# The end of an attention-and-spectral kernel: the last four row blocks copied and stored by ScalarE alone

## The chip, the core and the metric

The kernel runs on one core of a Trainium2 chip. A core has five engines that run side by side: TensorE (PE, matrix products), VectorE (DVE), ScalarE (ACT), GpSimd (POOL) and SyncE (SP, which here only issues DMA transfers and waits). Each engine works through its own list of instructions in order, and semaphores hold an engine back until another engine or a transfer has finished. The metric is device time in microseconds (us) for one execution of the whole program; lower is better.

## What is computed

The output has 2048 rows of 896 columns. The left 448 columns are multi-query attention, the right 448 a filter in the frequency domain:

```python
# A: 16 heads of 28, one key head and one value head
q = (x @ wq) split into heads;  k = x @ wk;  v = x @ wv
p = softmax(q @ k.T * 28 ** -0.5)
a = concat_heads(p @ v) @ wo                       # 2048 x 448
# B: 2-D real FFT, product with a complex filter, inverse
b = irfft2(rfft2(x) * (w_r + 1j * w_i))            # 2048 x 448
return concatenate([a, b], axis=-1)
```

## The kernel before

Attention is taken in four chunks of 512 query rows (`NC = 4`, `CW = 512`), in each chunk in four groups of four heads (`NG = 4`), and for each group over 16 blocks of 128 keys. A long list of steps, `PLAN`, sets by hand how scores (L891), exponentials (L826, L902, L916) and products with the values (L837) follow each other, and which pieces of the spectral half lie between them. The order of the instructions on PE, DVE and ACT is the order of the program's text in this part; SP's transfers stand in the order in which their data are made.

An output projection follows each chunk: a chunk's 512 rows are four row blocks of 128, and a row block's 128 x 448 result is a sum of products over the four head groups in one PSUM bank. For accuracy each factor is kept as a high and a low part, so that a group costs three products: high x high, low x high, high x low. For the first three chunks this work is spread through `PLAN`. The last chunk (`c = 3`) has nothing behind it, and its projection is the end of the program:

- `flush(kept)` (L948) makes the last products with the values; DVE transposes the result (L841).
- A loop over the four row blocks (L950 to L956) divides by the softmax sums and makes the high and low parts of the last head group, on DVE.
- `partial(k)` (L935) issues row block k's nine products over the head groups 0 to 2 (L745), which need nothing of that loop. `final(k)` (L939) issues its three products over group 3 (L942 to L944) and then calls `wo_out`.
- The order is partial 0, partial 1, final 0, partial 2, final 1, partial 3, final 2, final 3 (L957 to L963).
- `wo_out` (L747) copies the result from PSUM to an SBUF tile and stores it. With `last` from 1 to 3 (row blocks 0 to 2 here) ACT copies all 448 columns (L753) and SP issues the store (L757). With `last` 4 (row block 3) the columns are cut in two halves of 224: ACT copies the first and issues its store itself, DVE copies the second (L755) and SP issues that store.
- The SBUF tile `yb` has the tag `p0` or `p1` by turns, with one buffer each. So the copy of row block 2 must wait until the store of row block 0 has landed, and the copy of row block 3 until that of row block 1 has.

Behind this stands a branch (L968, L969): each of the five engines loads one number (`bits`, a bound on the scores, long known by then) into a register, compares it, and jumps over a slower fallback, L970 to L1035, which these data don't need. Behind the jump each engine waits for its own last work, and SP for all transfers and all engines, before the program ends (these instructions carry L969 and L1153).

Of the kernel before, what the change touches and what calls it, by code (L numbers as in the profile page):

```python
# [14 lines left out]
AF = mybir.ActivationFunctionType  # L15
# [5 lines left out]
S, D, H = 2048, 448, 16  # L21
# [48 lines left out]
def kernel(ctx: ExitStack, tc: tile.TileContext, t: dict):  # L70
    nc = tc.nc
# [73 lines left out]
    def fft1_a_mm(q, p):  # L145
        f, cs1 = ff[q], fc["cs1"][:113]
        pa = pair_of(bank())
        for e in range(2):
            for k, (n, o0) in enumerate(((113, 0), (112, 113))):
                for h in range(2):  # L150
                    for r in range(2):
                        r0 = 64 * h + 32 * r
                        mm(pa[r0:r0 + 32, e, o0:o0 + n], f[:, 2 * r + k, 2 * p + e, h], cs1[:, 2 * r + k, :n],  # L153
                           start=True, stop=True)
        return pa

    def fft1_a_out(q, p, pa):
        a = at1[q, p] = fp.tile([128, 2, DF], F32, name="a", tag=("pwr", "pwi")[p])
        return nc.scalar.activation(a, pa, AF.Copy)

    def fft1_b(q):
        return fft1_out(q, fft1_mm(q))
# [92 lines left out]
    with tc.tile_pool(name="w1", bufs=1) as w1:  # L255
# [37 lines left out]
        with tc.tile_pool(name="x1", bufs=2) as x1:  # L293
# [63 lines left out]
            def evac(c, g, pq):  # L357
                cs = slice(c * CW, (c + 1) * CW)
                out = nc.scalar.activation(qraw[:, g, cs], pq, AF.Copy)
                nc.vector.tensor_reduce(qmx[:, g, c:c + 1], qraw[:, g, cs], axis=AX.X, op=ALU.max,  # L360
                                        apply_absolute_value=True)
                return out
# [55 lines left out]
            for c in range(1, NC):  # L418
                for g in range(NG):
# [3 lines left out]
                    last = evac(c, g, pq)  # L423
# [43 lines left out]
        for p in range(2):  # L467
            last = fft1_a_out(6, p, fft1_a_mm(6, p))
# [7 lines left out]
        last = fft1_b(5)  # L476
# [26 lines left out]
    d, f, a, b, e, c = free  # L503
# [6 lines left out]
    def take():  # L510
        ready, bank = free.pop(free.index(min(free, key=lambda x: x[0])))
        clock["pe"] = max(clock["pe"], ready + 100)
        return bank
# [32 lines left out]
    def at_once(work=640, engine="dve"):  # L546
        clock[engine] = max(clock[engine], clock["pe"] + 200) + work
# [191 lines left out]
    def wo_mm(p, c, k, gs):  # L739
        s = slice(k * 128, k * 128 + 128)  # L740
        for g in gs:
            for n, (x, w) in enumerate(((oh, woh[:, g]), (ol, wox[:, g - 1] if g else woh[:, 0]), (oh, wol[:, g]))):
                if n == 1 and g == 0 and c < NC - 1:
                    continue
                mm(p, x[c][:, g, s], w, start=(g == 0 and n == 0), stop=(g == NG - 1 and n == 2))  # L745

    def wo_out(p, c, k, last=0):  # L747
        y = pp.tile([128, D], F32, name="yb", tag=f"p{k % 2}") if last else ap.tile([128, D], F32, name="ya")
        r0 = c * CW + k * 128
        for e in ((0, 1) if last == 4 else (0,)):  # L750
            s = slice(e * D // 2, (e + 1) * D // 2) if last == 4 else slice(0, D)
            if last and not e:
                nc.scalar.activation(y[:, s], p[:, s], AF.Copy)  # L753
            else:
                nc.vector.tensor_copy(y[:, s], p[:, s])  # L755
                at_once()
            (nc.scalar if last == 4 and not e else nc.sync).dma_start(t["oa"][r0:r0 + 128, s], y[:, s])  # L757

    wps = {}

    def wo_unit(c, k, g):
        if g == 0:
            wps[c, k] = take()
        p = wps[c, k][:, :D]
        need(("o", c, g))
        for x in (g,) if g == 0 else (g, g + NG - 1):
            need(("wo", x))
        wo_mm(p, c, k, (g,))
        passed(600 if g else 400)
        if g == NG - 1:  # L770
            wo_out(p, c, k)
            give(wps.pop((c, k)))
# [95 lines left out]
    for tokens in PLAN:  # L868
# [10 lines left out]
        for k in tokens:  # L879
# [9 lines left out]
            c, g, kc = steps[i if kind == "-" else n - 1 - i]  # L889
# [21 lines left out]
        for i in reversed(range(stay)):  # L911
# [5 lines left out]
            else:  # L917
                for h in hs:
                    p = keep[i][h // 2][:, h % 2]
# [12 lines left out]
    c = NC - 1  # L932
    ws = []

    def partial(k):  # L935
        ws.append(take()[:, :D])
        wo_mm(ws[k], c, k, range(NG - 1))

    def final(k):  # L939
        p, s = ws[k], slice(128 * k, 128 * k + 128)  # L940
        h, l = oh[c][:, NG - 1, s], ol[c][:, NG - 1, s]
        mm(p, h, woh[:, NG - 1], start=False, stop=False)  # L942
        mm(p, l, wox[:, NG - 2], start=False, stop=False)
        mm(p, h, wol[:, NG - 1], start=False, stop=True)  # L944
        wo_out(p, c, k, k + 1)


    flush(kept)  # L948
# [1 line left out]
    for k in range(4):  # L950
        divide(c, NG - 1, k)
        s = slice(128 * k, 128 * k + 128)
# [3 lines left out]
        nc.vector.tensor_tensor(ol[c][:, NG - 1, s], on[:, s], h.bitcast(F32), op=ALU.subtract)  # L956
    for k in (0, 1):  # L957
        partial(k)
    for k in (2, 3):
        final(k - 2)  # L960
        partial(k)
    final(2)
    final(3)  # L963


# [3 lines left out]
    with tc.If(rv > int(np.float32(BOUND).view(np.int32))), tc.tile_pool(name="g1", bufs=1) as g1:  # L969
# [32 lines left out]
        oa = t["oa"].rearrange("(n p) d -> n p d", p=128)  # L1002
        with tc.For_i(0, NC, 1) as nq:
            y = g1.tile([128, 4, D], F32, name="y")
            nc.vector.memset(y, 0.0)
            with tc.For_i(0, NG, 1) as ng:
# [5 lines left out]
                for i in range(4):  # L1012
# [3 lines left out]
                    with tc.For_i(0, 16, 1) as nk:  # L1016
# [5 lines left out]
                        p = g1.tile([128, CW], F32, name="pe")  # L1022
# [134 lines left out]
```

## Time and profile before

| | |
|---|---|
| median of three runs | 641.0 us (640.72 to 641.24) |
| the profiled execution | 640.4 us |
| its span, from the first to the last instruction | 638.6 us |
| busy time PE / ACT / DVE / POOL | 630.2 / 547.4 / 416.9 / 79.8 us |
| granted TensorE clock over the span | 0.998 of full speed |
| DMA traffic | 66.76 MB, 105 GB/s on average |

The page gives the busy time of each engine, the span in 40 slices, the chain of work that ended last, and the costliest groups of instructions. A chain row has a start, a length and the engine with the line, or a transfer. In other views of the trace a name with a q (SPq, ACTq, DVEq) means the engine's sequencer: register loads, branches, semaphore waits and the issuing of transfers, none of which count as busy time. In the timeline each row is a start, a length, an engine, a line and an operation with its tiles.

### The profile page before, as it was taken

To read this page: it belongs to the slowest core of one execution; us is meant where nothing else is said; L and a number is where in the kernel's file an instruction comes from. 1 tells how busy PE (TensorE), PEld (TensorE's weight loads), DVE (VectorE), ACT (ScalarE), POOL (GpSimd) and SP (SyncE) were. 2 spreads that over 40 slices of the span, in tenths; PEclk is the share of its full clock that TensorE was granted. 3 is DMA by queue.
4 is the path that set the end of the run, shared out by engine and by line. 5 is a ranking of instruction groups with operands and counts; after the bars stand their busy time and mean duration, and the time that the engine had idled before them with its cause. 6 is when DMAs were issued, how large, how long until landed. Compare 5 with 4: busy or idle time off the path is not lost.

```text
span 638.6 us, 12210 instructions
## 1 busy us (share of the span) xinstructions
PE 630.2 (99%) x4474; PEld 382.9 (60%) x4474; DVE 416.9 (65%) x756; ACT 547.4 (86%) x983; POOL 79.8 (12%) x150
## 2 busy tenths in 40 slices
PE   9999999999999999999999999999999999999995
PEld 7877655555555556655656566656655655555654
DVE  5999629889998934865755555585656343575632
ACT  5654999999999988988999998998999989899981
POOL 3022401011302110001120200011120200100010
PEclk9999999999999999999999999999999999999999
DMA  8765952636944613126341403034231503030001
GB/s 274 268 183 160 272 145 72 160 88 175 219 111 105 154 48 82 46 70 181 89 108 52 123 14 82 15 98 131 77 91 30 123 24 73 32 81 16 16 31 62
DMA packets 37699, 66.76 MB, mean 105 GB/s; under 512 B 7953, under 2 KB 23970, under 8 KB 36668
## 3 DMA queue, kind: packets, MB, share of 16 engines
q1 hardware_dynamic: 32848, 53.32, 29.5%
q0 software_dynamic: 4640, 12.48, 7.7%
q8 instruction: 36, 0.59, 0.4%
q14 instruction: 31, 0.25, 0.1%
q10 hardware_dynamic: 144, 0.11, 0.1%
HBM read 29.81 MB, written 17.89 MB: 75 GB/s over the span
## 4 chain that ended last, share of the span: by engine, by line
PE 98%; DMA 0%; ACT 0%; DVE 0%; issue 0%; ACTq 0%
PE s L891 30%; PE s L837 27%; PE s L355 6%; PE po L891 5%; PE sx L891 5%; PE po L837 4%; PE sx L837 4%; PE s L745 3%; PE s L153 2%; PE s L683 2%; PE s L669 2%; PE po L745 1%; PE sx L745 1%; PE pbb L172 1%; PE s L303 1%; DMA oa<-yb 0%
## 5 line engine op out<-in xcount | busy, mean ns | idle before, releaser
L826 ACT ACTIVATE p<-s 128x512 f32<-128x512 f32 x416 | 227.0, 640 | 22.9 <-PE s L891 20.4
L891 PE MATMUL s<-qa,ka 128*128 128x512 f32 x780 | 234.1, 405 | 0.0
L891 PEld LDWEIGHTS s<-qa,ka 128*128 128x128 f32 x780 | 142.0, 188 | 64.2 <-issue 30.2
L897 DVE COPY k<-s 128x512 f32<-128x512 f32 x128 | 84.1, 686 | 93.6 <-PE s L891 93.4
L837 PE MATMUL s<-p,vs 128*32 128x512 f32 x912 | 110.8, 594 | 0.0
L826 ACT ACTIVATE qraw<-s 128x512 f32<-128x512 f32 x150 | 84.3, 635 | 13.3 <-PE s L891 13.1
L916 ACT ACTIVATE k<-k 128x1024 f32<-128x1024 f32 x80 | 83.4, 1141 | 0.0
L837 PEld LDWEIGHTS s<-p,vs 128*32 128x32 f32 x912 | 28.0, 110 | 61.5 <-issue 58.8
L891 PE MATMUL po<-qa,ka 128*128 128x512 f32 x122 | 49.2, 403 | 0.0
L891 PE MATMUL sx<-qa,ka 128*128 128x512 f32 x122 | 48.9, 401 | 0.0
L826 ACT ACTIVATE p<-po 128x512 f32<-128x512 f32 x71 | 45.2, 637 | 1.6 <-PE po L891 1.3
L826 ACT ACTIVATE p<-sx 128x512 f32<-128x512 f32 x65 | 41.1, 632 | 4.1 <-PE sx L891 4.1
L837 PE MATMUL s<-qraw,vs 128*32 128x512 f32 x328 | 42.2, 595 | 0.0
L693 POOL TENSOR_TENSOR yo<-y 128x226 f32<-128x226 f32 x16 | 9.6, 598 | 240.3 <-issue 222.7
L837 PE MATMUL s<-k,vs 128*32 128x512 f32 x296 | 38.6, 594 | 0.0
L841 DVE STREAM_TRANSPOSE osb<-s 128x512 f32<-128x512 f32 x12 | 8.6, 715 | 37.9 <-PE s L837 37.8
L709 POOL DMA_DIRECT2D ol<-ol x36 | 18.2, 512 | 83.3 <-DVE ol L732 75.7
L891 PEld LDWEIGHTS sx<-qa,ka 128*128 128x128 f32 x122 | 22.9, 188 | 9.5 <-issue 4.2
L897 DVE COPY p<-s 128x512 f32<-128x512 f32 x41 | 27.3, 685 | 0.7 <-PE s L891 0.6
L891 PEld LDWEIGHTS po<-qa,ka 128*128 128x128 f32 x122 | 23.0, 188 | 7.9 <-ACT p L826 1.9
L916 ACT ACTIVATE p<-p 128x1024 f32<-128x1024 f32 x24 | 24.9, 1134 | 0.0
L355 PE MATMUL s<-xh,wqh 128*128 128x512 f32 x56 | 22.7, 405 | 0.0
(268 smaller groups left out, 942.9 us busy)
## 6 DMA issues: line engine op xcount, KB each, us to landing
qa<-qa SPq DMA_DIRECT2D x15, 512.0 KB
raw<-xa SPq DMA_DIRECT2D x16, 256.0 KB
xb<-xb SPq DMA_DIRECT2D x8, 512.0 KB
qa<-qh SPq DMA_DIRECT2D x64, 64.0 KB
qa<-ql SPq DMA_DIRECT2D x60, 64.0 KB
ob<-yo SPq DMA_DIRECT2D x16, 226.0 KB
t<-bs SPq DMA_DIRECT2D x16, 225.0 KB
wr<-wr POOLq DMA_DIRECT2D x16, 225.0 KB, 4.2
```

What stands on the lines that cost most here:

```text
L153: mm(pa[r0:r0 + 32, e, o0:o0 + n], f[:, 2 * r + k, 2 * p + e, h], cs1[:, 2 * r + k, :n], start=True, stop=True)
L355: mm(pq, w[:, j, gs], x[:, j], start=(j == 0 and n == 0), stop=(j == 3 and n == 1))
L669: mm(pz[:w, j], c2["c", q][:, j, o0:o0 + w], c2["F", q][:, j], start=True, stop=True)
L683: mm(py[:, k], z[:w, r, js], cs3[:w, k], start=True, stop=True)
L693: nc.gpsimd.tensor_tensor(yo[:, 0:2], y1[:, 0], y1[:, 1], op=ALU.add)
L709: nc.gpsimd.dma_start(ol[c][o, g].bitcast(F32), ol[c][r, 0].bitcast(F32))
L745: mm(p, x[c][:, g, s], w, start=(g == 0 and n == 0), stop=(g == NG - 1 and n == 2))
L826: nc.scalar.activation(tiles[-1][:, h % 2], sc, AF.Exp, scale=SCALE)
L837: mm(po[c, g][32 * i:32 * i + 32], vs[:, kc], ps[i // 2][:, i % 2], start=(n == 1), stop=(n == 16))
L891: begun.append(mm(sc, ka[:, kc * 128:(kc + 1) * 128], qa[c, g][:, h], start=True, stop=True))
L897: nc.vector.tensor_copy(keep[i][h // 2][:, h % 2], sc)
L916: nc.scalar.activation(p, p, AF.Exp, scale=SCALE)
```

## The change

For the last chunk `wo_out` no longer cuts the fourth row block in two. ACT copies every one of the four row blocks in one piece of 448 columns and issues every one of the four stores. DVE copies nothing there any more, and SP issues no store there any more. `partial(3)`, the nine products of the fourth row block, moves behind `final(2)`, the last three products of the third. The tags of `yb`, the branch and all that stands before are the same.

```diff
-    def wo_out(p, c, k, last=0):
+    def wo_out(p, c, k, last=False):
         y = pp.tile([128, D], F32, name="yb", tag=f"p{k % 2}") if last else ap.tile([128, D], F32, name="ya")
         r0 = c * CW + k * 128
-        for e in ((0, 1) if last == 4 else (0,)):
-            s = slice(e * D // 2, (e + 1) * D // 2) if last == 4 else slice(0, D)
-            if last and not e:
-                nc.scalar.activation(y[:, s], p[:, s], AF.Copy)
-            else:
-                nc.vector.tensor_copy(y[:, s], p[:, s])
-                at_once()
-            (nc.scalar if last == 4 and not e else nc.sync).dma_start(t["oa"][r0:r0 + 128, s], y[:, s])
+        if last:
+            nc.scalar.activation(y, p, AF.Copy)
+        else:
+            nc.vector.tensor_copy(y, p)
+            at_once()
+        (nc.scalar if last else nc.sync).dma_start(t["oa"][r0:r0 + 128], y)
...
-        wo_out(p, c, k, k + 1)
+        wo_out(p, c, k, True)
...
     for k in (0, 1):
         partial(k)
-    for k in (2, 3):
-        final(k - 2)
-        partial(k)
+    final(0)
+    partial(2)
+    final(1)
     final(2)
+    partial(3)
     final(3)
```

## The prediction

> **What bounds the kernel now.** I read the page first: busy times, and the two queues that fetch instructions (packets, MB, share).
>
> ```profile
> span 638.6 us, 12210 instructions
> PE 630.2 (99%) x4474; PEld 382.9 (60%) x4474; DVE 416.9 (65%) x756; ACT 547.4 (86%) x983; POOL 79.8 (12%) x150
> q8 instruction: 36, 0.59, 0.4%
> q14 instruction: 31, 0.25, 0.1%
> ```
>
> PE is busy for 99% of the span, and the change leaves PE's instructions the same in number and kind. What can change is the stretch after PE's last product. So next come the chain of waits for the last 11 us, and the timeline's rows of PE's last product, DVE's last step on the four row blocks and SP's last issues before them.
>
> ```profile
> 628.37 0.55 ACT yb L753
> 628.92 0.02 issue
> 628.94 3.08 DMA oa<-yb
> 632.02 0.02 issue
> 632.04 0.04 ACTq L753
> 632.08 0.05 issue
> 632.12 0.37 ACT yb L753
> 632.49 0.02 issue
> 632.51 0.39 DVE yb L755
> ```
>
> ```profile
> 612.61 2.67 SPq L696 DMA_DIRECT2D ob<-yo  x2
> ...
> 627.05 0.29 DVE L956 TENSOR_TENSOR ol<-osb,oh 128x128 fp32r<-128x128 f32 x1
> ...
> 630.75 0.37 PE L943 MATMUL po<-wox,ol 128*128 128x448 f32 x1
> ...
> 630.79 0.55 ACT L753 ACTIVATE yb<-s 128x448 f32<-128x448 f32 x1 [1.88 <-PE s L944]
> 630.95 0.36 PE L944 MATMUL po<-wol,oh 128*128 128x448 f32 x1
> ```
>
> Two things are to be seen. PE ends at 630.95 + 0.36 = 631.31, but the copy of row block 3 starts at 632.12: it waits for its tile, whose former content (row block 1) is stored from 628.94 to 632.02. And the chain ends with DVE's half copy at 632.51 + 0.39 = 632.90, though the span ends at 638.6: 5.7 us are no engine's work. They are sequencers, and these rows show them: the load of the branch's number (L968), the branch and what follows it (L969), the end (L1153), and what SP waited for (two answers of the waits view).
>
> ```profile
> L968 ACTq TENSOR_LOAD <-bits x1: 477/477/477, 632.9 to 632.9; - x1
> L968 SPq TENSOR_LOAD <-bits x1: 517/517/517, 633.3 to 633.3; - x1
> ```
> ```profile
> L969 SPq EVENT_SEMAPHORE  x6: 17/17/17, 636.5 to 636.9; - x6
> L969 POOLq COMPARE_BRANCH  x1: 54/54/54, 614.4 to 614.4; - x1
> ...
> L969 DVEq COMPARE_BRANCH  x1: 72/72/72, 633.1 to 633.1; - x1
> L969 ACTq COMPARE_BRANCH  x1: 54/54/54, 633.5 to 633.5; - x1
> L969 SPq COMPARE_BRANCH  x1: 50/50/50, 633.9 to 633.9; - x1
> L969 ACTq EVENT_SEMAPHORE  x1: 17/17/17, 633.9 to 633.9; - x1
> L969 DVEq EVENT_SEMAPHORE  x1: 21/21/21, 636.0 to 636.0; - x1
> ```
> ```profile
> L1153 SPq EVENT_SEMAPHORE  x14: 17/28/28, 637.0 to 638.6; - x14
> ...
> L1153 POOLq DRAIN  x3: 50/108/8986, 614.9 to 638.4; - x3
> L1153 SPq DRAIN  x3: 7/7/13, 637.7 to 638.1; - x3
> ```
> ```profile
> SPq L969 <- SPq L969: 2.6, 1, 2.6
> ```
>
> SP jumps at 633.9 and does its next instruction 2.6 us later, at 636.5; from there it needs 2.1 us to the end (638.6). DVE, with nothing to wait for but its own copy, stands still as long: 633.1 + 0.07 to 636.0, 2.8 us. ACT stands still for 0.4 (633.5 to 633.9), and so does POOL (614.4 to 614.9). In the built program POOL's jump is 213 and ACT's 214 instructions wide, SP's 256 and DVE's 309: the two wide jumps cost 2.6 to 2.8 us, the two narrow ones 0.4. I take the long gaps for instructions that are not there yet. So the end is bound by **SP's late branch**: SP branches only after it has issued row block 3's half store at 632.9, which waits for DVE's half copy, which waits for ACT's.
>
> **The change part by part.** Durations and the rates of the stores come from these rows of the tile `yb` and of the windows view (length, then busy time of PE, PEld, DVE, ACT, POOL, then the clock, DMA share and GB/s).
>
> ```profile
> L757 SPq DMA_DIRECT2D oa<-yb x4: 332/332/333, 626.5 to 632.9; - x4
> L753 ACT ACTIVATE yb<-s x2: 544/545/546, 628.4 to 630.8; 128x448 f32<-128x448 f32 x2
> ...
> L753 ACT ACTIVATE yb<-po x1: 357/357/357, 632.1 to 632.1; 128x224 f32<-128x224 f32 x1
> L757 ACTq DMA_DIRECT2D oa<-yb x1: 376/376/376, 632.5 to 632.5; - x1
> ```
> ```profile
> 627.50:628.00 0.50, 0.50 (x4) 0.46 (x4) 0.00 (x0) 0.00 (x0) 0.00 (x0) 1.00 0.97 358
> 628.00:628.50 0.50, 0.50 (x4) 0.47 (x3) 0.00 (x0) 0.13 (x1) 0.00 (x0) 1.00 0.03 7
> ...
> 631.00:631.50 0.50, 0.31 (x2) 0.00 (x0) 0.00 (x0) 0.34 (x1) 0.00 (x0) 1.00 0.07 22
> 631.50:632.00 0.50, 0.00 (x0) 0.00 (x0) 0.00 (x0) 0.00 (x0) 0.00 (x0) 1.00 0.00 0
> ```
>
> *PE's order.* Row block 2's three last products come nine products earlier, so its copy can start some 1.8 us sooner (nine at 0.2, the step from 630.75 to 630.95), but ACT must first issue row block 1's store (0.376 from 628.94). The copy then runs at about 629.4 instead of 630.79, and its store's issue is over by 630.4. Neither was late: with the old order copy and issue would end by 631.8, still ahead of 632.02. PE's last product stays at 631.31, since the number of products ahead of it is the same and DVE has made all it needs by 627.05 + 0.29. I cost this edit at nothing; if row block 1's store landed early, it would keep copy 2 out of the way of copy 3.
>
> *Row block 1's store.* It moves from SP to ACT, behind the same copy (628.37 to 628.92). Issued at 628.94 by either; ACT's issue takes 0.376 against 0.332. The transfer itself is slow here: row block 0's store, issued at 626.5, has nearly all its bytes through by 628.0, 1.5 us later, while row block 1's still has a share of 0.07 (one engine of 16) moving after 631.0. That one engine is held by something outside the change (PE branches at this time, and q8 fetches 16 KB in a piece: 0.59 MB in 36). I leave the landing at 632.02.
>
> *Row block 3's copy.* Start 632.12 as before. One piece of 448 columns, 0.55, replaces ACT's 0.37 and DVE's 0.39 one after the other: the copy ends at 632.67, 0.23 earlier than DVE's half did.
>
> *Row block 3's store.* Issued at 632.69 by ACT, over at 633.07. No full store of this queue is in the trace. From row block 0's: 1.5 us to the end of the bytes, and 0.5 more until the landing is told (row block 1's bytes end by 631.5, its landing is 632.02); with the 0.04 of the longer issue 2.0 us, landing at 634.7. Bounds: 1.7 if the half block's bytes set it, 3.08 as row block 1's. I take 2.0, the undisturbed one.
>
> *SP's branch.* SP loses four issues and two waits. Its last transfers before them are those of L696, over at 612.61 + 2.67 = 615.3. It then loads its number (0.517), branches by about 616 and has its instructions by 618.6, sixteen microseconds before they matter. The 2.6 us gap goes out of the end altogether. DVE likewise: its last work is at 627.34, its jump over by 630.9.
>
> *ACT's branch* is now the last. After the issue at 633.07: load and branch, 0.64 in before (632.89 to 633.53), to 633.7, and with its narrow gap of 0.4 it is through at 634.1, covered by the store's landing at 634.7. ACT's program has six instructions more ahead of the branch; the jump is still 214 wide.
>
> *The tail.* SP now stands in its final list when the store lands. In the built program this list has twelve waits (637.0 to 637.7 in before, 0.06 each) and row block 3's landing is the eighth, at 637.4: from there to 638.6 are 1.2 us. Bounds: 0.9 (from the drain at 637.7) and 2.1 (the whole list from 636.5).
>
> Sum: 632.12 + 0.55 + 0.02 + 2.0 + 1.2 = 635.9 against 638.6, **2.7 us less**. The profiled execution took 640.4 with its span of 638.6; the median of the runs is 641.0. Taken off the median: **638.3**.
>
> A rule of the Trainium skill bears on the gaps: "Runtime: NRT & Kernel Launch", section "Instruction fetch mechanics", says that a taken branch to a place outside the two blocks held forces a fetch first. SP's 2.6 us against ACT's 0.4 agree. The same section gives blocks of 256 instructions for all engines but PE; the q14 row above has 0.25 MB in 31 packets, 8 KB each, which is half such a block. By the skill's size SP's jump of 256 would stay inside two blocks from every place and its gap would have no cause, so the trace's size is the one that fits; the sum is 638.3 by either, but rival A below is possible by the trace's size alone.
>
> **The rivals.**
>
> *A: ACT's jump becomes a long one.* 8 KB are 128 of the built program's instructions of 64 bytes. If two such blocks are held, a jump of 214 stays inside them only from the first 42 places of a block. ACT was there in before (gap 0.4); six instructions more would push it out from 6 of these 42 places. Then ACT stands 2.6 to 2.8 us from 633.7, to 636.4, and SP's last wait, for ACT, leaves 0.96 (637.68 to 638.64): 637.3 to 637.5, a gain of 1.2 to 1.4, 639.6 to 639.8. By the Trainium skill's section above this would be ACT's fetch. Chance 0.12.
>
> *B: row block 1's store escapes its delay.* On another queue its bytes may pass the 16 KB fetch. Copy 3 would start behind PE's end, at 631.4, 0.7 earlier: 637.6. Against it: the issue is at the same moment, and the windows show a single count of 16 engines for all queues. Chance 0.06.
>
> *C: the change doesn't do what I read in it: SP's gap isn't its jump but the end of the last store.* If a store's end blocked SP until 636.5, 3.6 us after the issue at 632.9, the same after the issue at 632.69 gives 636.3 and a gain of 0.2: 640.8. For it: the gap lies right behind the store. Against it: DVE shows the same gap and issues no store. Chance 0.10.
>
> *D, slower: ACT's queue lands full blocks late.* The trace has one store on it, of half a block. A lateness of d enters twice, since row block 1's landing releases copy 3 and row block 3's landing releases SP. From d = 1.35 us the 2.7 are used up; at d = 2, twice the whole undisturbed store, the time is 638.3 + 4.0 = 642.3. Against it: ACT's issue is hardly longer than SP's (0.376 against 0.332), and the bytes go through the same engines. Chance 0.10.
>
> **How the numbers follow.** My forecast gets 0.62: 638.3. Its own ends: tail 0.9 instead of 1.2 gives 638.0; a store of 3.08 instead of 2.0 gives 639.4. Range 637.5 to 639.9: with B at the lower end and A at the upper it holds 0.80; C and D are left out. A measurement of this kernel can tell about 0.2% (1.3 us) from no change. Faster by more, below 639.7: the forecast, B and half of A, 0.74. Within: C and the other half of A, 0.16. Slower: D, 0.10.
>
> **What would show it.** In the profile after: SP's compare and branch near 616 and its gap there; ACT's copy of row block 3 at 632.1 for 0.55; ACT's gap behind its branch 0.4 (A: over 2.5); SP's final drains 1 us after the store's landing, near 635. It would be wrong if the copy of row block 3 started away from 632.1, or if SP still did its L969 waits at 636.

## The result, and the profile after

The changed kernel takes 637.6 us (median of six runs, 637.4 to 638.16) against 640.86 for the kernel before (six runs, 640.47 to 641.75): a ratio of 0.9949, 95% interval 0.9936 to 0.9962. That is 3.3 us less, between 2.4 and 4.1 by the interval. Forecast were 2.7 us less and 638.3 us; the time is 0.7 under that and lies inside the range (637.5 to 639.9).

The profiled execution took 637.73 us, 636.0 of them its span (forecast 635.9, from 638.6). The page, with the queue of PE's instruction fetches:

```profile
span 636.0 us, 12208 instructions
...
q8 instruction: 36, 0.59, 0.4%
```

The timeline of the changed kernel's end (start, length, engine, line, operation with its tiles, and the idle time before it with its releaser):

```profile
628.45 0.54 ACT L751 ACTIVATE yb<-s 128x448 f32<-128x448 f32 x1 [1.82 <-DMA oa<-yb]
...
629.02 0.34 ACTq L755 DMA_DIRECT2D oa<-yb  x1
...
629.47 0.55 ACT L751 ACTIVATE yb<-s 128x448 f32<-128x448 f32 x1 [0.47 <-PE s L942]
...
630.04 1.06 ACTq L755 DMA_DIRECT2D oa<-yb  x1
...
631.09 0.36 PE L942 MATMUL po<-wol,oh 128*128 128x448 f32 x1
632.24 0.54 ACT L751 ACTIVATE yb<-po 128x448 f32<-128x448 f32 x1 [2.23 <-SPq L968]
632.82 0.34 ACTq L755 DMA_DIRECT2D oa<-yb  x1
```

PE ends at 631.09 + 0.36 = 631.45. Row block 3's copy still starts only at 632.24, in one piece now, and its store is issued at 632.82. The releaser in brackets isn't to be trusted: SP and ACT wait for the same landing, SP's wait ended 4 ns earlier (632.176 against 632.180 in the trace), and the view names SP. The chain of waits breaks off at the same place, which leaves it with three pieces:

```profile
632.19 0.00 ACTq L751
632.20 0.04 issue
632.24 0.54 ACT yb L751
```

What released both is the landing of row block 1's store, whose last part comes at 632.16. In before the same wait was put down to the transfer. The branch, the end, and what SP waited for (three views of the changed kernel; PEldq is PE's sequencer):

```profile
L968 SPq EVENT_SEMAPHORE  x6: 17/17/17, 628.7 to 632.5; - x6
...
L968 SPq COMPARE_BRANCH  x1: 50/50/50, 616.1 to 616.1; - x1
L968 DVEq COMPARE_BRANCH  x1: 72/72/72, 628.1 to 628.1; - x1
L968 PEldq COMPARE_BRANCH  x1: 361/361/361, 628.3 to 628.3; - x1
L968 DVEq EVENT_SEMAPHORE  x1: 21/21/21, 631.1 to 631.1; - x1
...
L968 ACTq COMPARE_BRANCH  x1: 54/54/54, 633.7 to 633.7; - x1
L968 ACTq EVENT_SEMAPHORE  x1: 17/17/17, 634.2 to 634.2; - x1
```

```profile
L1152 SPq EVENT_SEMAPHORE  x14: 17/28/28, 632.5 to 635.9; - x14
...
L1152 SPq DRAIN  x3: 7/7/13, 635.1 to 635.4; - x3
```

```profile
SPq L1152 <- DMA oa<-yb: 1.8, 2, 1.3
```

SP branches at 616.1, twelve microseconds before its first wait behind the branch ends (628.7), and DVE at 628.1: it stands still for 3 us as before, but nobody waits for it. ACT's gap, now the last one, is 0.4 (633.7 to 634.2). SP, which in before stood still at 634 without its next instruction, now waits for a transfer: row block 3's store lands at 634.75, 1.94 us after its issue, and SP's next row starts at 634.77, 1.2 us ahead of the end (635.97).

### The profile page after: what moved, and what is told of

Same layout as the page of the kernel before. It is cut to its first block, busy times and chain, and to the rows that moved or that the text cites. A ratio compares the mean times of both kernels' runs of the same rounds, so it can differ in the third digit from the quotient of the medians.

```text
span 636.0 us, 12208 instructions
## 1 busy us (share of the span) xinstructions
PE 630.3 (99%) x4474; PEld 383.0 (60%) x4474; DVE 416.8 (66%) x755; ACT 547.4 (86%) x983; POOL 79.6 (13%) x150
```

## The experiments

The time up to PE's last product differs from one execution to the next by as much as some of the effects looked for. That product ends at 631.31 in before, at 632.18 in e1 and at 632.77 in e3, with the same number of products before it. So the profiles are compared by the **tail**: the span's end less the end of PE's last product. Before it is 638.64 - 631.31 = 7.3 us, in the changed kernel 635.97 - 631.45 = 4.5. So 2.8 us are gained behind PE's last product, and nothing ahead of it.

The theory is the prediction's: SP's late branch, which has to wait for its instructions, set the end. The rivals are its C (the gap is the end of the last store) and A (another engine's jump can take its place), and that the new order on PE or the copy in one piece brought the gain.

| kernel | what differs | us | ratio to before (95%) | PE's end | span | tail |
|---|---|---|---|---|---|---|
| after | | 637.60 | 0.9949 (0.9936 to 0.9962) | 631.45 | 636.0 | 4.5 |
| e1 | before with the new order alone | 641.37 | 1.0003 (0.9994 to 1.0012) | 632.18 | 639.7 | 7.5 |
| e2 | after, last store by SP | 640.67 | 0.9992 (0.9983 to 1.0001) | 631.78 | 638.6 | 6.8 |
| e3 | after, DVE copies half of the last block | 640.33 | 0.9987 (0.9978 to 0.9996) | 632.77 | 638.8 | 6.0 |
| e4 | before, SP's branch 73 places later in the program | 640.23 | 0.9987 (0.9978 to 0.9996) | 631.72 | 638.2 | 6.5 |
| e5 | after, ACT's branch 76 places later | 639.92 | 0.9977 (0.9967 to 0.9988) | 632.50 | 638.4 | 5.9 |
| e6 | after, four tiles | 637.57 | 0.9944 (0.9931 to 0.9958) | 632.54 | 636.3 | 3.8 |
| e7 | before without branch and fallback | 637.03 | 0.9932 (0.9918 to 0.9945) | 631.55 | 635.3 | 3.8 |
| e8 | after without branch and fallback | 637.42 | 0.9942 (0.9929 to 0.9956) | 631.75 | 635.4 | 3.7 |
| e9 | after again | 638.47 | 0.9951 (0.9937 to 0.9965) | 632.53 | 637.0 | 4.5 |
| e10 | four tiles again | 637.58 | 0.9946 (0.9932 to 0.9959) | 632.00 | 635.8 | 3.8 |
| e11 | four tiles, old order | 637.84 | 0.9949 (0.9935 to 0.9962) | 631.61 | 635.7 | 4.1 |
| e12 | before, four tiles | 641.14 | 0.9997 (0.9988 to 1.0006) | 631.77 | 638.5 | 6.8 |

Each ratio goes by before's own runs beside it (e1 to e4: 641.24, e5 to e8: 641.17, e9 to e12: 641.35).

### e1: the new order alone

```diff
-    for k in (2, 3):
-        final(k - 2)
-        partial(k)
+    final(0)
+    partial(2)
+    final(1)
     final(2)
+    partial(3)
     final(3)
```

> The kernel before with only the new order of PE's products (the fourth row block's nine behind the third's last three). My theory, SP's late branch: the last copy, the half stores and SP's branch keep their places, so the span stays at 638.6 us as before, within 0.3 us. If the order were the source of the gain, the span would be near 636.0.

SP's branch and its next instruction in e1 (the rows of the branch's line):

```profile
L970 SPq EVENT_SEMAPHORE  x6: 17/17/17, 637.6 to 638.0; - x6
...
L970 SPq COMPARE_BRANCH  x1: 50/50/50, 634.8 to 634.8; - x1
```

The gap of 2.7 us is there (634.87 to 637.61), and the time is that of before. The order alone is worth nothing. The span came out at 639.7 and not at the expected 638.6; of these 1.1 us 0.9 lie ahead of PE's end and 0.2 behind it.

### e2 and e3: the last store or half the last copy given back

```diff
-        (nc.scalar if last else nc.sync).dma_start(t["oa"][r0:r0 + 128], y)
+        (nc.scalar if last and k < 3 else nc.sync).dma_start(t["oa"][r0:r0 + 128], y)
```

> The changed kernel, but row block 3's store is issued by SP again, in one piece behind ACT's one copy. Theory of SP's late branch: SP issues at about 632.8, branches at 633.8, stands 2.6 us, needs 2.1 us from there: span 638.5, nearly all of the 2.6 us lost. Rival, the gain comes from the one copy in place of two halves one after the other: the copy is as short as in the changed kernel, so the span is 636.0.

The branch in e2, and SP's one store from its timeline:

```profile
L968 SPq EVENT_SEMAPHORE  x6: 17/17/17, 636.5 to 636.9; - x6
...
L968 SPq COMPARE_BRANCH  x1: 50/50/50, 634.0 to 634.0; - x1
```

```profile
632.98 0.33 SPq L755 DMA_DIRECT2D oa<-yb  x1
```

One store moved back to SP, and SP branches behind it at 634.0 and stands until 636.5. The tail goes from 4.5 to 6.8: 2.3 of the 2.8 us are lost again by this one instruction's place.

```diff
-        if last:
+        if last and k == 3:
+            nc.scalar.activation(y[:, :D // 2], p[:, :D // 2], AF.Copy)
+            nc.vector.tensor_copy(y[:, D // 2:], p[:, D // 2:])
+        elif last:
```

> The changed kernel, but the second half of row block 3 is copied by DVE behind ACT's half, and ACT stores the block in one piece. SP keeps its early branch. The theory that a late branch costs its engine's gap: now DVE's branch is late (load beside its copy at about 632.6, first instruction behind the jump near 636.1), and SP, waiting for DVE in its last list, ends 1.1 us later: span 637.2. Rival, only the two copies one after the other cost: landing near 635.0 and 1.2 us of tail, span 636.2.

The branch in e3:

```profile
L971 DVEq COMPARE_BRANCH  x1: 72/72/72, 634.3 to 634.3; - x1
...
L971 DVEq EVENT_SEMAPHORE  x1: 21/21/21, 637.7 to 637.7; - x1
```

DVE takes over SP's part: it branches behind its half copy and stands from 634.4 to 637.7, and SP waits for it at the end. The tail is 6.0, as expected from 637.2 less 631.3; the expected span was missed because PE ended 1.5 us later in this execution than in before. That all of the last block's work went to one engine is thus not a detail: a late DVE costs 1.5 us of the tail, a late SP 2.3.

### e4 and e5: the same branch at another place in the program

If the gaps are instructions that aren't there, they must depend on where the branch lies among the blocks that are fetched, and on nothing that the kernel computes. Empty instructions shift the branch: 73 on SP in before, 76 on ACT in after, both early enough not to be waited for.

```diff
+    for _ in range(73):
+        behind(nc.sync.drain(), begun[-1])
```

> The kernel before with 73 empty drains on SP ahead of its last stores, while SP is idle; they only move SP's branch to another place in its program. Theory that SP's 2.6 us are a fetch of instructions that lie outside the two blocks of 128 held: from near the start of a block SP's jump stays inside them, SP's gap falls to about 0.4, and then DVE's own gap (first instruction at 636.0) ends the program: span 637.1. Rivals: a jump as wide as SP's always costs 2.6, or the gap is the end of its store: span 638.6 as before.

The branch in e4, and SP's waits:

```profile
L971 SPq EVENT_SEMAPHORE  x6: 17/17/17, 634.9 to 635.3; - x6
...
L971 DVEq COMPARE_BRANCH  x1: 72/72/72, 633.6 to 633.6; - x1
...
L971 SPq COMPARE_BRANCH  x1: 50/50/50, 634.4 to 634.4; - x1
...
L971 DVEq EVENT_SEMAPHORE  x1: 21/21/21, 636.7 to 636.7; - x1
```

```profile
SPq L971 <- SPq L971: 0.5, 1, 0.5
```

SP jumps over the same 256 instructions, behind the same half store, and its 2.6 us are 0.5. So it is neither the width of the jump alone nor the store: rival C falls. The whole kernel gained less than was expected (tail 6.5, not 5.8). DVE's gap, until then covered, comes next (633.7 to 636.7), but SP stops once more within its final list, from 635.83 to 637.09 by the trace, and this ends last. An 8 KB fetch began at 635.42. That SP had run off the end of the block it had jumped into fits this; the records don't say for which engine a fetch was made, so it isn't shown.

The run shows that the place of the branch decides, and not by which rule. The rule as the prediction counts it can't be the whole: a jump of 256 places leaves two blocks of 128 from every place, and yet this one came through in 0.45 us. In the built program 35 of the 256 places are labels, marks of where the fallback's blocks begin; without them the jump is 221 wide, which two blocks can hold. That is a reading of the file, and no run tests it.

```diff
+    for _ in range(76):
+        nc.scalar.drain()
```

> The changed kernel with 76 empty drains on ACT while it is idle ahead of its last copies; they only move ACT's branch, the jump is as wide as before. From PE's last product to the end of the span the changed kernel needs 4.5 us. Theory of blocks held: from this place ACT's jump leaves them, ACT's gap grows from 0.4 to 2.6 to 3.0, and SP's last wait, for ACT, ends 1 us before the end: 5.9 to 6.3 us, 1.4 to 1.8 us slower than the changed kernel. Rival, the width of the jump decides: gap 0.4, 4.5 us as before.

The branch in e5, and what SP waited for at the end:

```profile
L970 ACTq COMPARE_BRANCH  x1: 54/54/54, 634.9 to 634.9; - x1
L970 ACTq EVENT_SEMAPHORE  x1: 17/17/17, 637.4 to 637.4; - x1
```

```profile
SPq L1154 <- ACTq L970: 1.3, 1, 1.3
```

The other way round: ACT's gap of 0.4 becomes 2.5 with its jump as wide as before, SP waits for ACT, and 1.4 us of the gain are gone. Rival A's mechanism exists; the change just didn't reach it. The rule in the Trainium skill, "Runtime: NRT & Kernel Launch", section "Instruction fetch mechanics", that a taken branch out of the two pages held waits for a fetch, agrees with both runs: 2.6 to 0.5, 0.4 to 2.5.

### e7 and e8: no branch at all

Both leave out the branch and the fallback behind it (the lines from `a, b, d = spare` to the fallback's end).

```diff
-    a, b, d = spare
-    rv = nc.values_load(bits.bitcast(I32)[0:1, 0:1])
-    with tc.If(rv > int(np.float32(BOUND).view(np.int32))), tc.tile_pool(name="g1", bufs=1) as g1:
...
```

> The kernel before without the branch and the fallback behind it (the check of the bound on the scores is left out; these data don't need it). Theory: without a jump nobody waits for instructions; SP issues its last store, stands in its final list, the store lands 3.3 us behind PE's last product and 1.2 us later the program ends: 4.5 us instead of 7.3, 2.8 us faster than before. Rival, the end is bound by the stores and copies: 7.3 us still, less 0.6 for the load and the compare.

> The changed kernel without the branch and the fallback. Theory: in the changed kernel the jumps are all covered by the last store, so leaving them out changes nothing: 4.5 us from PE's last product to the end, and the same time as the changed kernel. Rival, ACT's load and branch behind the last store still cost: 0.5 to 1 us faster than the changed kernel.

Without a branch the two kernels take the same time (637.03 and 637.42, overlapping intervals; tails 3.8 and 3.7): so nearly all that the change brought is bound to the branch. But both tails are shorter than the 4.5 that was expected, and e8 contradicts the theory in one point: I had taken every jump in the changed kernel to be covered. The page and the timeline of e8:

```profile
q8 instruction: 35, 0.57, 0.4%
```

```profile
630.34 0.34 ACTq L755 DMA_DIRECT2D oa<-yb  x1
...
631.39 0.36 PE L942 MATMUL po<-wol,oh 128*128 128x448 f32 x1
631.79 0.54 ACT L751 ACTIVATE yb<-po 128x448 f32<-128x448 f32 x1 [1.48 <-PE po L942]
```

And the windows of the changed kernel, then of e7 (length, busy time of PE, PEld, DVE, ACT, POOL, clock, DMA share, GB/s):

```profile
630.50:631.00 0.50, 0.50 (x4) 0.47 (x3) 0.00 (x0) 0.00 (x0) 0.00 (x0) 1.00 0.09 18
631.00:631.50 0.50, 0.45 (x3) 0.07 (x1) 0.00 (x0) 0.00 (x0) 0.00 (x0) 1.00 0.05 14
```

```profile
630.50:631.00 0.50, 0.50 (x5) 0.46 (x4) 0.00 (x0) 0.00 (x0) 0.00 (x0) 1.00 0.27 97
631.00:631.50 0.50, 0.50 (x3) 0.17 (x1) 0.00 (x0) 0.47 (x1) 0.00 (x0) 1.00 0.00 0
```

PE jumps too (its branch at 628.3 stands among the rows of the branch above), and 16 KB are fetched on its queue (36 fetches, here 35). In the changed kernel that fetch runs from 629.38 to 630.73, beside row block 1's store: 15 of the store's 16 parts have landed by 630.99, the last comes at 632.16. In the windows one engine of 16 is still busy (share 0.05) when nothing else moves. Without PE's jump the bytes of e7's store are through by 631.0, and in e8 the copy of row block 3 starts 0.04 us behind PE's end instead of 0.79. So PE's jump costs the changed kernel 0.7 to 0.8 us. e7 and e8 leave out the other engines' jumps as well, but the times single out PE's. In all twelve profiles with the branch the store's last part lands 1.39 to 1.43 us behind the end of this fetch (here 632.16 - 630.73), wherever the fetch lies; in e7 and e8 it lands 0.01 us behind the fifteenth. The records don't name the DMA engine of a packet; that store and fetch share one is inferred from these times.

### e6, e9 and e10: four tiles

If that is so, a copy that needn't wait for row block 1's store should win the 0.7 us without touching the branch.

```diff
-        y = pp.tile([128, D], F32, name="yb", tag=f"p{k % 2}") if last else ...
+        y = pp.tile([128, D], F32, name="yb", tag=f"p{k}") if last else ...
```

> The changed kernel with four tiles for the last four copies instead of two, so that the fourth copy doesn't wait for the second block's store. Theory: that wait is now on the path; the copy starts 0.1 us behind PE's last product instead of 0.8, everything after it moves with it: 3.8 us from PE's last product to the end, 0.7 us faster than the changed kernel. Rival, the engines' branches (ACT's among them) already end the program: 4.5 us, no change.

The timeline of e6:

```profile
632.18 0.36 PE L942 MATMUL po<-wol,oh 128*128 128x448 f32 x1
632.58 0.54 ACT L751 ACTIVATE yb<-po 128x448 f32<-128x448 f32 x1 [1.52 <-PE po L942]
```

The copy follows PE by 0.04 us, and the tail is 3.8, as short as without any branch. e9 (the changed kernel) and e10 (e6) were taken side by side to see whether the timed runs show it:

> The changed kernel itself, beside the three others of this set on one chip. From PE's last product to the end 4.5 us as in its first profile, and 0.4 to 0.5% faster than before.

> The changed kernel with four tiles for the last copies, again, beside the changed kernel. Tail 3.8 us, 0.7 us (0.1%) faster than the changed kernel; whether the timed runs can tell 0.1% is open.

The tails came out the same again, 4.5 and 3.8. The times, 638.47 and 637.58, lie the right way round, but their intervals overlap; 0.7 us is 0.1%, which these runs don't settle. In the profiles four tiles beat both kernels; in time they are better than before by intervals clear of 1 (e6 0.9944, e10 0.9946), and not surely better than the change.

### e11 and e12: what the order and the tiles are worth apart

e11 is e6 with the old order of the products, e12 is before with the four tiles.

```diff
-    final(0)
-    partial(2)
-    final(1)
+    for k in (2, 3):
+        final(k - 2)
+        partial(k)
     final(2)
-    partial(3)
     final(3)
```

> Four tiles and ScalarE alone, but the old order of PE's products (the fourth block's nine before the third's last three). Theory: with the tile wait gone ACT itself is next. The third copy starts 0.5 us ahead of PE's last product and takes 0.55, its store's issue 0.34 to 1.1 behind it, so the fourth copy starts 0.4 to 1.1 us behind PE's last product instead of 0.05: tail 4.1 to 4.9 us instead of 3.8. Rival, the order is worth nothing here either: 3.8.

> The kernel before with four tiles for the last copies and nothing else. Theory: the wait for the tile goes (0.7 to 0.8 us), but SP's late branch and its 2.6 us stay: tail 6.5 us instead of 7.3, 0.1% faster than before. Rival, the wait for the tile is what the changed kernel saved: tail near 4.5.

The timeline of e11:

```profile
631.04 0.54 ACT L751 ACTIVATE yb<-s 128x448 f32<-128x448 f32 x1 [1.88 <-DMA oa<-yb]
...
631.25 0.37 PE L942 MATMUL po<-wol,oh 128*128 128x448 f32 x1
631.61 0.34 ACTq L755 DMA_DIRECT2D oa<-yb  x1
632.00 0.54 ACT L751 ACTIVATE yb<-po 128x448 f32<-128x448 f32 x1 [0.41 <-PEq L967]
```

With the old order row block 2's copy and issue end at 631.95, and the last copy comes 0.39 us after PE's end (631.61) instead of 0.04. So the new order is worth 0.3 us (tail 3.8 against 4.1), but only once the tile's wait is gone; with two tiles the copy of row block 3 waits longer for the landing. e12 shows the other half: SP stands still for 2.7 us (633.7 to 636.4), and four tiles in before leave the time where it was. Its tail is 0.5 shorter than before's, less than the timed runs can show and less than the 0.8 expected: the copy loses its wait, and SP branches 0.6 sooner behind PE's end, but stands 0.1 longer (2.67 against 2.58).

## Why the prediction was right

Point by point, by its own steps:

- **PE's order at nothing**: right in this change. e1 shows it directly (1.0003), and e11 shows the condition that the prediction named, copy 2 out of the way of copy 3, with its price of 0.3 us. One time in this step was off: row block 2's issue was over at 631.10, not by 630.4, still ahead of 632.12.
- **Row block 1's store, landing left at 632.02**: 632.16, in an execution 0.14 us later at PE's end. The delay was taken from the profile and put down to one engine held at the time of PE's fetch; e7 and e8 bear that out. Rival B (the store escapes it) didn't happen, and its price of 0.7 was right: e6 and e10 show it.
- **Row block 3's copy, 0.55 in one piece from 632.12**: 0.54 from 632.24. Its end is 0.12 earlier than DVE's half copy was, and 0.25 earlier when both are counted from PE's end (1.34 against 1.59).
- **Row block 3's store, 2.0 from issue to landing**: 1.94. ACT's queue is no slower than SP's (row block 0's store: 1.99 on ACT, 1.93 on SP in before), and rival D falls.
- **SP's branch at 616, its gap out of the end**: 616.1. This is the term that carries the sum. e2 takes away 2.3 of the 2.8 us by giving SP one store back, e4 takes SP's gap away inside the kernel before (though only 0.8 of the tail with it, since SP then stops elsewhere), and with no branch (e7, e8) the change does nothing. The other 0.5 is e2's tail against before's. By the rows 0.4 of it is that SP's branch is done sooner behind PE's end (634.02 - 631.78 against 633.96 - 631.31): half of that is the shorter copy in one piece, the other half its earlier start in this execution. The rest is a gap of 2.48 in place of 2.58. No run measured these parts alone.
- **ACT's narrow gap of 0.4, covered**: 0.41, over by 634.2, before the landing at 634.75. Rival A had a true mechanism (e5), and that it stayed away here is partly luck: nothing in the change chose ACT's place, and another place would have cost 1.4 us. The condition that gave A its chance, 42 places, counts widths and blocks as in SP's case, where e4 contradicts that count; so no run supports the 0.12.
- **The end, 1.2 behind the landing**: 1.20.
- **The size**: in the profiled executions 638.64 - 635.97 = 2.7 us less, as forecast; by the tail 2.8. The timed medians differ by 3.3; 2.7 lies in their interval (2.4 to 4.1). The other 0.6 is accounted for by which executions were profiled: before's ran 0.5 under its median (640.4 against 640.86), the changed kernel's 0.1 over (637.73 against 637.6). The forecast of 638.3 was 0.7 too long: by these 0.6, and by 0.1 for the base (641.0 from three runs).

What failed was in the theory's use later, not in the forecast: the expectations of e7 and e8 left out that PE's own jump, by its fetch, still reached the end through a tile's buffer.

## What to carry to other kernels

When a program ends with a branch, look in the sequencers' rows for the time between each engine's branch and its next instruction: an engine with a long gap there should get its last work early, and the late work belongs to an engine with a short one (here 0.4 against 2.5 to 3.3 us); instructions added ahead of the branch can swap these roles (73 and 76 did here). Compare such ends from the last instruction that both kernels share, since here the stretch before it differed between executions by up to 1.5 us, about half of what the change brought. And give the last few tiles buffers of their own: two buffers made the last copy wait for a store that something else had slowed down.

## What had not been expected of the hardware

- **An issue that starts beside PE's fetch ends late.** ACT's issue of row block 2's store took 1.06 us in the changed kernel against 0.34 to 0.38 for its others, and 0.34 in e8, where PE's fetch is gone. Eight profiles have such an issue, 0.78 to 1.49 us long (in e1 on SP), and in each it ended 0.37 us behind the fetch's end. The held store alone doesn't do it: in before and in e11 this issue came after the fetch and took 0.33 and 0.34, with row block 1's store still open. It hid here, since copy 3 came later anyway. Why the fetch holds an issue is open.
- **A jump can cost twice**: e4's SP came through its branch in 0.45 us and stood still for 1.26 us in the straight code behind it; that this was the end of a block is not shown.
- **Gaps by engine**: 2.5 to 2.7 us on SP (e2 2.48, e1 2.74), 2.5 on ACT (e5), 2.8 to 3.3 on DVE (before 2.8, e3 3.28), and 0.4 to 0.5 for the short ones (ACT and POOL in before, SP in e4).
